# Two query tiles of 128 at the start of batch 0, with the other queries of that batch loaded later

## The chip, the cores and the metric

The kernel runs on one core of one Trainium2 chip. The metric is the device time of one execution in microseconds (us). Engines: PE is TensorE, DVE VectorE, ACT ScalarE, POOL GpSimd, SP SyncE.

## The reference

Block-sparse attention feeds a feed-forward layer. Shapes: q, k, v are 4 x 8 x 768 x 64 (batch, heads, sequence, head size), w_in is 512 x 2048, w_out 2048 x 512, all float32.

```python
scores = q @ k.T / sqrt(64)               # per batch and head
mask: neighbouring blocks of 32, first and last block, 3 random key blocks per query block
attn = softmax(where(mask, scores, -1e9)) @ v
x = attn, tokens x 512                    # 3072 tokens
out = relu(x @ w_in) ** 2 @ w_out
```

## The kernel before

Work goes by unit: two heads of one batch, so four units per batch, sixteen in all. A *slot* is one group of scores (256 queries, two key chunks of 128, two heads), with its exponential on ACT, its mask on DVE and its value matmuls on PE. When the four units of a batch have a query tile, the feed-forward layer ("hidden" matmuls with w_in, "output" matmuls with w_out) of these tokens can run. PE has some 258 us of matmuls, so the kernel is good in so far as PE is never without work.

The order of instructions on every engine is fixed when the kernel is built, by a list scheduler in Python. I call its result the **plan**. It always takes the task that can start first, by durations and arrival times that are written into the source. Nothing on the chip changes the order later: if the plan believes a load to be there and it comes later, the engine waits at that place.

The arrival times of batch 0, the weights, and the gates that hold batch 1 back behind weights (cut):

```python
    LEAD = 14                                   # casts of a later unit at most so far ahead
    PACE0, PACE, ... = 44, 1.313, ...           # slot s of batches 1..3 not before PACE0 + PACE * (s - first)
    ...
    load(0, (sy, sc_, sy)); load(1, (sc_, sy, sc_)); load(2, (sy, sc_, sy)); load(3, (sc_, sy, sy))
    ...
    def loads_gate(i, e):                       # a tiny DMA that reads weight chunk i, on the Sync queue
        src = w_in_sb[...] if i < NWP else w_out_sb[...]
        sy.dma_start(out=scratch[0:1, i % 4:i % 4 + 1], in_=src)
    ...
    arrive = [(6.2, 6.2, 8.4), (8.4, 10.5, 10.5), (12.5, 12.5, 13.6), (13.6, 15.2, 16.3)]   # q, k, v of units 0..3
    ...
        if u >= HP:                             # units of later batches: behind a gate
            g = gate[2] if u == HP else gate[5] if u == HP + 1 else gate[7]
            ld_t = T_(("SP", 1.3), s0 - 30, load, u, (sy, sy, sy), deps=... + [g], dma=4.0)
    ...
        if u == HP - 1:                         # weights: chunks 0..3 are w_in, 4..7 are w_out, 2.65 us each
            for i in range(2 * NWP):
                wl[i] = T_(("POOL", 0.85), -50 + i, w_load, i, after=12.6, late=2.2, dma=2.65)
            for i in (2, 5, 7):
                gate[i] = T_(("SP", 0.2), i, loads_gate, i, deps=[wl[i]], late=0.0)
```

The softmax here doesn't subtract the row's maximum and nothing guards it: scores larger than these inputs give would overflow.

Of the kernel before, what the change touches and what calls it, by code (L numbers as in the profile page):

```python
# [19 lines left out]
P = 128  # L20
# [5 lines left out]
def kernel(  # L26
# [31 lines left out]
    N_WARM = 12  # L58
# [21 lines left out]
    AHEAD = {"PE": 0, "DVE": 0, "ACT": 0.2, "POOL": 0.0, "SP": 0.0}  # L80
    LEAD = 14
    PACE0, PACE, SINGLE, MASK_AT = 44, 1.313, 1, 12.0
# [116 lines left out]

    sy, sc_ = nc.sync, nc.scalar  # L200
    sb_i = consts.tile([nb, n_rand * 2], I32, name="sb_i")
    sy.dma_start(out=sb_i, in_=sampled_blocks.bitcast(I32))
    load(0, (sy, sc_, sy))
    load(1, (sc_, sy, sc_))
    load(2, (sy, sc_, sy))
    load(3, (sc_, sy, sy))
# [7 lines left out]
    warm = consts.tile([P, 512], BF, name="warm")  # L214
# [7 lines left out]
    for _ in range(N_WARM):  # L222
        nc.tensor.matmul(junk, warm[:, 0:P], warm, start=True, stop=True)  # L223
# [7 lines left out]
    G.iota(row, pattern=[[0, 1]], base=0, channel_multiplier=1, **small)  # L231
    o3 = oh.rearrange("a (n p) -> a n p", p=P)
# [4 lines left out]
    identb = consts.tile([P, P], BF, name="identb")  # L237
    make_identity(nc, identb)
# [19 lines left out]
    A.copy(out=oh[D:P, :], in_=oh[0:D, :])  # L258
# [13 lines left out]
    def mask_rows(e):  # L272
        mtile["R"] = ps_s.tile([P, 1024], F32, name="pb", tag="ps")
        for c0 in (0, 512):
            w = min(512, S - c0)
            nc.tensor.matmul(mtile["R"][:, c0:c0 + w], bm, oh[0:nb, c0:c0 + w], start=True, stop=True)

    def mask_rows_evac(c0, c1, e):
        copy(e, R2[:, c0:c1], mtile["R"][:, c0:c1])
# [47 lines left out]

    def w_load(i, e):
        if i == 0:
            G.tensor_copy(out=held, in_=raw[2][1][0:1, 0, 0, 0:2])  # L330
        if i < NWP:
            fs = slice(i * d_ff // NWP, (i + 1) * d_ff // NWP)
            G.dma_start(out=w_in_sb[:, :, fs], in_=wiv[:, :, fs])
        else:
            ns = slice((i - NWP) * NF // NWP, (i - NWP + 1) * NF // NWP)
            G.dma_start(out=w_out_sb[:, ns, :], in_=wov[:, ns, :])
# [12 lines left out]
    def scores(slots, add, e):  # L349
        for a in slots:  # L350
            u, qi, cp = a
            i = u % NPB
            ps = ps_s.tile([P, 2, 2, QW], F32, name="ps", tag="ps")
            qsl = slice(qi * QW, (qi + 1) * QW)
            for c in range(2):
                ksl = slice((cp * 2 + c) * P, (cp * 2 + c + 1) * P)
                for h in range(2):
                    hs = slice(h * D, (h + 1) * D)
                    nc.tensor.matmul(ps[:, h, c, :], QK[i][hs, 1, ksl], QK[i][hs, 0, qsl],  # L359
                                     start=c == 0, stop=not add, skip_group_check=True)  # L360
                for h in range(2) if add else ():
                    hs = slice(h * D, (h + 1) * D)
                    nc.tensor.matmul(ps[:, h, c, :], oh[hs, ksl], R2[hs, qsl],  # L363
# [3 lines left out]
    def exps(a, e):  # L367
        pT = work.tile([P, 2, 2, QW], BF, name="pT", tag="pT", bufs=PT_BUFS)
        A.activation(out=pT, in_=stile.pop(a), func=AF.Exp, scale=scale)  # L369
        ptile[a] = pT  # L370

    def masks(a, e):
        u, qi, cp = a
        pT = ptile[a]
        m = MK[:, cp * 2:cp * 2 + 2, qi * QW:(qi + 1) * QW]
        V.tensor_tensor(out=pT, in0=pT, in1=m[:, None].broadcast_to([P, 2, 2, QW]), op=AOP.mult)  # L376

    def outs_of(t):
        return t[:, 0:4 * VW].rearrange("p (c h d) -> p c h d", h=2, d=VW)

    def values(a, e):
        u, qi, cp = a
        i = u % NPB
        pT = ptile.pop(a)
        if cp == 0:
            otile[u, qi] = ps_o.tile([P, 512], F32, name="po", tag="po")
        po = outs_of(otile[u, qi])
        for c in range(2):
            n = cp * 2 + c
            for qc in range(2):  # L390
                for h in range(2):
                    nc.tensor.matmul(po[:, qc, h, :], pT[:, h, c, qc * P:(qc + 1) * P], VT[i][:, h, n, 0:VW],  # L392
# [3 lines left out]
    def normalize(u, qi, e):  # L396
        po = outs_of(otile[u, qi])
        rs = work.tile([P, 2, 2, 1], F32, name="rs", tag="rs")
        V.reciprocal(out=rs, in_=po[:, :, :, D:VW])  # L399
        xq = work.tile([P, 2, 2, D], BF, name="xq", tag="xq", bufs=XQ_BUFS)  # L400
        V.tensor_tensor(out=xq, in0=po[:, :, :, 0:D], in1=rs.broadcast_to([P, 2, 2, D]), op=AOP.mult)  # L401
        xtile[u, qi] = xq

    def x_transp(u, qi, e):
        xq = xtile.pop((u, qi))
        pt = otile[u, qi][:, 384:512].bitcast(BF)
        for qc in range(2):
            nc.tensor.transpose(pt[:, qc * P:(qc + 1) * P], xq[:, qc].rearrange("p h d -> p (h d)"), identb)  # L408

    def x_evac(u, qi, e):  # L410
# [3 lines left out]
        copy(e, xT[b][:, a, qi * QW:(qi + 1) * QW], otile.pop((u, qi))[:, 384:512].bitcast(BF))  # L414

    def x_transp_dma(u, qi, e):
        b, a = divmod(u, HP)
        if b not in xT:
            xT[b] = work.tile([P, HP, S], BF, name="xT", tag="xT", bufs=XT_BUFS)
        sy.dma_start(out=xT[b][:, a, qi * QW:(qi + 1) * QW].rearrange("r (c p) -> r c p", p=P),  # L420
                     in_=xtile.pop((u, qi)).rearrange("p c h d -> p (c h d)"), transpose=True)
        otile.pop((u, qi))
# [4 lines left out]
    TILES = [(0, qi * QW, QW) for qi in range(NQ)]  # L427
    TILES += [(b, c0, S // 2) for b in range(1, B) for c0 in (0, S // 2)]
    NY = 8

    def hidden(T, f, half, e):
        b, c0, w = T
        if half == 0:
            htile[T, f] = ps_h.tile([P, TWM], F32, name="ph", tag="h")[:, 0:w]
        ph = htile[T, f]
        for kc in range(half * KM // 2, (half + 1) * KM // 2):
            nc.tensor.matmul(ph, w_in_sb[:, kc, f * P:(f + 1) * P], xT[b][:, kc, c0:c0 + w],  # L437
                             start=(kc == 0), stop=(kc == KM - 1))

    def relu(T, f, e):  # L440
        r = work.tile([P, TWM], F32, name="r", tag="r", bufs=R_BUFS)[:, 0:T[2]]
# [7 lines left out]
    def square(T, f, e):  # L449
        g = work.tile([P, TWM], BF, name="g", tag="g", bufs=G_BUFS)[:, 0:T[2]]  # L450
# [5 lines left out]
        gtile[T, f] = g  # L456
# [33 lines left out]
    def T_(engs, key, f, *args, **kw):  # L490
        return Task(engs, key, (lambda e: f(*args, e)), **kw)

    arrive = [(6.2, 6.2, 8.4), (8.4, 10.5, 10.5), (12.5, 12.5, 13.6), (13.6, 15.2, 16.3)]

    order = [(a, qi, cp) for qi in range(NQ) for a in range(HP) for cp in range(CP)]
    order += [(b * HP + a, qi, cp) for b in range(1, B) for qs in ((0, 1), (2,)) for a in range(HP) for qi in qs
              for cp in range(CP)]
    first = {}
    for s, (u, qi, cp) in enumerate(order):
        first.setdefault(u, s)  # L500
    ev, cv, tr, sc_of, va_of, mu, mk, wl, gate, xb = {}, {}, {}, {}, {}, {}, {}, {}, {}, {}

    def prepare(u):
# [5 lines left out]
        if u >= HP:  # L509
# [4 lines left out]
            for w in (1, 0):  # L514
                qc = Buf("qc")
                c = T_({"DVE": 0.55, "POOL": 1.2}, 101, cast_qk, u, w, slice(0, NCH), bias={"POOL": 0.5}, get=[qc], port=True,
                       after=PACE0 + PACE * (s0 - HP * NQ * CP) - LEAD, **at)
                tr[u].append(c)
                ev[u][w, 0] = ev[u][w, 2] = T_(("SP", 1.0), s0 - 10, transp_dma, u, w, deps=[c] + old_s, put=[qc], dma=1.2)
        else:  # L520
            at = dict(after=arrive[u][2])
            for ns in (slice(0, 2), slice(2, NCH)) if u == 0 else (slice(0, NCH),):
                n = ns.stop - ns.start
                for w in (0, 1):
                    qc, hb = Buf("qc"), Buf("h")
                    opts = {"ACT": 0.23 + 0.1 * n} if u == 0 and w else {"DVE": 0.07 + 0.08 * n}
                    if u:
                        opts["POOL"] = 1.2
                    c = T_(opts, s0 - 6 + ns.start, cast_qk, u, w, ns, after=arrive[u][w], get=[qc], port=True)
                    tr[u].append(c)  # L530
# [162 lines left out]
```

## Time and profile before

| | before |
|---|---|
| time, median of 3 runs | 276.78 us (276.52 to 277.39) |
| span of the profiled run | 275.2 us |
| PE busy | 263.5 us, 96% |
| mean granted TensorE clock | 0.998 |

Full PE means that the opening decides.

The measure of this study is the **delay** that the prediction defines: the real start of every fourth slot's scores minus the PE work that stands ahead of it in PE's order, priced from the trace. In an idle-free stretch it is flat; a wait of PE raises it. So the delay at PE's end, plus PE's work, plus a tail of some 3 us, is the span. Narrow slots are counted by area, so that "slot 12", the twelfth, stands at the same amount of scores in all kernels. A delay is that of the one profiled execution, a time that of all executions.

### The profile page before, as it was taken

The page shows a single profiled execution, that of the slowest core. Times are in us where ns is not written, and L with a number is a line of the kernel's source. Part 1 is how long each engine was busy: PE and PEld are TensorE (multiplying, and loading weights), DVE is VectorE, ACT ScalarE, POOL GpSimd, SP SyncE. Part 2 cuts the span into 40 slices and gives each one's busy share as a digit, 9 for nine tenths or more (in the row PEclk, how much of TensorE's full clock was granted, in tenths as well). Part 3 has the DMA queues.
Part 4 walks back from the last instruction along what each step waited for, and adds up shares of the span by engine and source line. Part 5 has one row for each costly group of instructions (what it writes and reads, how often), then busy time and mean ns, then how long its engine had stood idle before and what let it go on. Part 6 is the DMA issues. An engine that isn't in the chain of part 4 may idle for free.

```text
span 275.2 us, 7001 instructions
## 1 busy us (share of the span) xinstructions
PE 263.5 (96%) x2812; PEld 156.7 (57%) x2850; DVE 198.0 (72%) x392; ACT 212.0 (77%) x315; POOL 77.3 (28%) x105
## 2 busy tenths in 40 slices
PE   7897999899999999999999999999999999999994
PEld 2565756567666655655555555555555655555543
DVE  6794799989989778898987768876876745444400
ACT  4688999899899799997898988889989743444311
POOL 4660655625441224453232420111110100010010
PEclk9999999999999999999999999999999999999999
DMA  7999997999979969413512611111022011111122
GB/s 251 376 233 206 267 278 252 262 280 285 318 104 255 206 174 247 154 57 69 117 48 48 137 21 50 57 21 49 12 60 58 12 48 39 40 38 38 40 76 76
DMA packets 50522, 36.89 MB, mean 134 GB/s; under 512 B 30906, under 2 KB 47546, under 8 KB 50490
## 3 DMA queue, kind: packets, MB, share of 16 engines
q1 hardware_dynamic: 44906, 30.29, 41.3%
q0 software_dynamic: 4224, 4.19, 9.2%
q10 hardware_dynamic: 1360, 1.97, 2.1%
q8 instruction: 22, 0.36, 0.5%
q14 instruction: 10, 0.08, 0.1%
HBM read 27.26 MB, written 6.29 MB: 122 GB/s over the span
## 4 chain that ended last, share of the span: by engine, by line
PE 87%; DVE 4%; ACT 3%; DMA 2%; issue 2%; POOL 1%; POOLq 0%; ACTq 0%
PE ph L437 28%; PE py L477 28%; PE po L392 14%; PE ps L359 12%; DMA vs<-in_v_dram 2%; ACT pT L369 2%; PE junk L223 2%; DVE pT L376 1%; PE pt L311 1%; DVE r L446 1%; POOL g L455 1%; DVE QK L182 1%; PE po L408 1%; PE ps L363 0%; ACT MK L291 0%
## 5 line engine op out<-in xcount | busy, mean ns | idle before, releaser
L369 ACT ACTIVATE pT<-ps 128x1024 bf16<-128x1024 f32 x144 | 139.2, 1022 | 9.0 <-PE ps L359 5.6
L437 PE MATMUL ph<-xT,w_in_sb 128*128 128x384 bf16 (+1 forms) x576 | 107.0, 308 | 0.2
L376 DVE TENSOR_TENSOR pT<-pT,MK 128x1024 bf16<-128x1024 bf16 x132 | 98.8, 769 | 10.5 <-ACT pT L369 10.3
L477 PE MATMUL py<-w_out_sb,g 128*128 128x512 bf16 (+1 forms) x362 | 96.2, 369 | 2.5 <-POOL g L455 0.9
L455 POOL TENSOR_TENSOR g<-r 128x256 bf16<-128x256 f32 (+1 forms) x59 | 50.0, 853 | 164.5 <-DVE r L446 134.6
L437 PEld LDWEIGHTS <-w_in_sb 128*128 128x128 bf16 x576 | 51.9, 97 | 33.0 <-issue 1.3
L446 DVE TENSOR_SCALAR r<-ph 128x384 f32<-128x384 f32 (+1 forms) x96 | 49.6, 519 | 28.5 <-PE ph L437 27.2
L453 ACT ACTIVATE g<-r 128x384 bf16<-128x384 f32 (+1 forms) x85 | 42.3, 501 | 29.2 <-DVE r L446 28.5
L392 PEld LDWEIGHTS <-pT 128*128 128x128 bf16 x1152 | 44.4, 98 | 22.4 <-issue 7.7
L392 PE MATMUL po<-VT,pT 128*128 128x65 bf16 x1152 | 53.9, 194 | 1.5 <-DVE xT L182 0.7
L477 PEld LDWEIGHTS <-g 128*128 128x128 bf16 x400 | 36.3, 97 | 24.7 <-POOL g L455 1.2
L359 PE MATMUL ps<-QK 64*128 64x256 bf16 x576 | 46.6, 272 | 0.1
L359 PEld LDWEIGHTS <-QK 64*128 64x128 bf16 x576 | 22.8, 94 | 24.1 <-issue 20.7
L444 ACT ACTIVATE r<-ph 128x384 f32<-128x384 f32 (+1 forms) x48 | 21.0, 445 | 5.3 <-PE ph L437 4.7
L401 DVE TENSOR_TENSOR xq<-po,rs 128x256 bf16<-128x256 f32 x48 | 20.4, 424 | 1.7
L399 DVE RECIPROCAL rs<-po 128x4 f32<-128x4 f32 x48 | 8.6, 180 | 17.9 <-PE po L392 17.6
L180 ACT COPY ys<-py 128x512 f32<-128x512 f32 (+1 forms) x21 | 11.9, 565 | 11.7 <-PE py L477 11.7
L182 POOL CAST VT<-vs 128x768 bf16<-128x768 f32 x15 | 13.5, 902 | 17.9 <-PE po L392 12.1
L182 DVE CAST qc<-ks 128x768 bf16<-128x768 f32 x14 | 9.5, 682 | 0.0
L182 DVE CAST qc<-qs 128x768 bf16<-128x768 f32 (+2 forms) x13 | 8.6, 666 | 0.8 <-DMA qs<-in_q_dram 0.8
L363 PE MATMUL ps<-R,oh 64*128 64x256 bf16 x48 | 5.9, 269 | 0.0
L223 PE MATMUL junk<-warm 128*128 128x512 bf16 x12 | 4.2, 528 | 1.5 <-DVE warm L215 1.5
(52 smaller groups left out, 61.3 us busy)
## 6 DMA issues: line engine op xcount, KB each, us to landing
out_dram<-ys SPq DMA_DIRECT2D x23, 256.0 KB, 2.2
vs<-in_v_dram SPq DMA_DIRECT2D x15, 384.0 KB, 6.4
qs<-in_q_dram SPq DMA_DIRECT2D x14, 384.0 KB, 4.5
ks<-in_k_dram SPq DMA_DIRECT2D x14, 384.0 KB, 6.4
w_in_sb<-in_moe_w_in_dram POOLq DMA_DIRECT2D x4, 512.0 KB, 10.1
w_out_sb<-in_moe_w_out_dram POOLq DMA_DIRECT2D x4, 512.0 KB, 20.7
ks<-in_k_dram ACTq DMA_DIRECT2D x2, 384.0 KB, 6.0
qs<-in_q_dram ACTq DMA_DIRECT2D x2, 384.0 KB, 5.0
```

What stands on the lines that cost most here:

```text
L182: (V if e == "DVE" else G).tensor_copy(out=out, in_=in_)
L359: nc.tensor.matmul(ps[:, h, c, :], QK[i][hs, 1, ksl], QK[i][hs, 0, qsl], start=c == 0, stop=not add, skip_group_check=True)
L369: A.activation(out=pT, in_=stile.pop(a), func=AF.Exp, scale=scale)
L376: V.tensor_tensor(out=pT, in0=pT, in1=m[:, None].broadcast_to([P, 2, 2, QW]), op=AOP.mult)
L392: nc.tensor.matmul(po[:, qc, h, :], pT[:, h, c, qc * P:(qc + 1) * P], VT[i][:, h, n, 0:VW], start=(n == 0 and qc == 0 and h == 0), stop=n ...
L401: V.tensor_tensor(out=xq, in0=po[:, :, :, 0:D], in1=rs.broadcast_to([P, 2, 2, D]), op=AOP.mult)
L437: nc.tensor.matmul(ph, w_in_sb[:, kc, f * P:(f + 1) * P], xT[b][:, kc, c0:c0 + w], start=(kc == 0), stop=(kc == KM - 1))
L444: A.activation(out=r, in_=src, func=AF.Relu)
L446: V.tensor_scalar(out=r, in0=src, scalar1=0.0, scalar2=None, op0=AOP.max)
L453: A.activation(out=g, in_=r, func=AF.Square)
L455: (G if e == "POOL" else V).tensor_mul(out=g, in0=r, in1=r)
L477: nc.tensor.matmul(ytile[T, i], gtile[T, f][:, ts * P:(ts + 1) * P], w_out_sb[:, f, cs[0]:cs[1]], start=(f == 0), stop=(f == NF - 1))
```

## The change

The intent: start earlier and have feed-forward work for PE earlier. The first 256 queries of batch 0 are treated as two tiles of 128, each slot with three key chunks instead of two; their feed-forward work can start after eight short slots. So that they come early, only these queries are loaded with the keys and values; the remaining 512 queries of the four units (**late queries** below) are loaded behind the values of unit 3, beside the weights. With it go the plan's arrival times, its pace, and a number that sends more squares to GpSimd. The core (warm-up, order of constants, generalised helper functions cut):

```diff
-    AHEAD = {"PE": 0, "DVE": 0, "ACT": 0.2, "POOL": 0.0, "SP": 0.0}
-    LEAD = 14
-    PACE0, PACE, SINGLE, MASK_AT = 44, 1.313, 1, 12.0
+    AHEAD = {"PE": 0.05, "DVE": 0, "ACT": 0.2, "POOL": 0.0, "SP": 0.0}
+    LEAD = 8
+    PACE0, PACE, SINGLE, MASK_AT = 36, 1.611, 1, 12.0
...
-    load(0, (sy, sc_, sy))
-    load(1, (sc_, sy, sc_))
-    load(2, (sy, sc_, sy))
-    load(3, (sc_, sy, sy))
+    for eng, u, w, ns in ((sc_, 0, 1, KEYS[0]), (sy, 0, 0, QRS[0]), (sc_, 1, 1, ALL), (sy, 0, 1, KEYS[1]),
+                          (sc_, 1, 0, QRS[0]), (sy, 0, 2, ALL), (sc_, 1, 2, ALL), (sy, 2, 1, ALL),
+                          (sy, 2, 0, QRS[0]), (sy, 3, 1, ALL), (sy, 3, 0, QRS[0]), (sy, 2, 2, ALL), (sy, 3, 2, ALL)):
+        load_part(eng, u, w, ns)
...
+    def load_rest(e):
+        sy.dma_start(out=scratch[0:1, 3:4], in_=raw[HP - 1][2][0:1, 0, 0, 0:1].bitcast(BF)[:, 0:1])
+        for u in range(HP):
+            load_part(sy, u, 0, QRS[1])
...
-    TILES = [(0, qi * QW, QW) for qi in range(NQ)]
+    QT = {0: [(0, P), (P, P)] + [(c0, QW) for c0 in range(QW, S, QW)]}
+    QT.update({b: [(c0, QW) for c0 in range(0, S, QW)] for b in range(1, B)})
+    TILES = [(0, c0, w) for c0, w in QT[0]]
...
-    arrive = [(6.2, 6.2, 8.4), (8.4, 10.5, 10.5), (12.5, 12.5, 13.6), (13.6, 15.2, 16.3)]
+    arrive = {(0, 1, 0): 4.3, (0, 0, 0): 4.4, (0, 1, CP): 5.3, (0, 2, 0): 7.4, (1, 1, 0): 6.7, (1, 0, 0): 7.4, (1, 2, 0): 9.5,
+              (2, 1, 0): 9.6, (2, 0, 0): 10.0, (3, 1, 0): 11.1, (3, 0, 0): 11.5, (2, 2, 0): 12.5, (3, 2, 0): 13.5}
+    arrive.update({(u, 0, 2): 17.0 + 0.9 * u for u in range(HP)})      # the late queries
...
+            T_(("SP", 2.0), -60, load_rest, after=13.5)
             for i in range(2 * NWP):
-                wl[i] = T_(("POOL", 0.85), -50 + i, w_load, i, after=12.6, late=2.2, dma=2.65)
+                wl[i] = T_(("POOL", 0.85), -50 + i, w_load, i, after=9.6 + 2.6 * i, late=1.3, dma=3.9 if i in (1, 2) else 2.6)
...
-                sq_of[x] = T_(SQ[w], n_key, square, t, f, deps=[rr], get=[gb], put=[rb], bias={"ACT": 0.2})
+                sq = T_(SQ[w], n_key, square, t, f, deps=[rr], get=[gb], put=[rb], bias={"ACT": 0.7})
```

## The prediction

> **What bounds the kernel now.** I read the busy shares first, then the chain of waits over the whole span, then the chain in the opening, then the DMA queues.
>
> From the page (busy us, share of the span, instructions; then the share of each engine in 40 slices of 6.9 us):
>
> ```profile
> PE 263.5 (96%) x2812; PEld 156.7 (57%) x2850; DVE 198.0 (72%) x392; ACT 212.0 (77%) x315; POOL 77.3 (28%) x105
> ...
> PE   7897999899999999999999999999999999999994
> ...
> DMA  7999997999979969413512611111022011111122
> ```
>
> PE is full from about 55 us on; its weak slices are the first eight, and there DMA is full too. A stretch of the chain of waits at 140 us (start, us, what) shows what "full" means:
>
> ```profile
> 141.14 0.86 PE py L477 x4
> 142.00 0.65 PE ph L437 x4
> 142.65 0.54 PE ps L359 x8
> ...
> 145.73 0.54 PE ps L359 x8
> 146.28 0.59 PE po L392 x16
> ```
>
> Pieces follow each other without a gap. They give PE's price list: an output matmul (512 columns) 0.215 us, a hidden one (384 columns) 0.162, a two-slot score group 0.54 and its 16 value matmuls 0.59, both including the change between 64-row and 128-row use of the array. Hidden matmuls of 256 columns start 0.109 apart in the timeline, transposes 0.056.
>
> I priced both PE instruction orders with this list (score matmuls in concurrent pairs; score and value groups split so that they give the 0.54 and 0.59 above, about 0.115 per change of row mode). Before: 258.5 us of PE work. Comparing the running sum with the real start of every fourth slot's scores gives a **delay** (real time minus PE work due so far): 7.7 us at slot 4, 8.2 at slot 12, 10.5 at slot 24, 13.0 at slot 36, and then 12.95 to 13.0 for all 108 slots left. So after 55 us nothing but PE work counts, and span = 258.5 + 13.0 + 3.5 (last copy and store; PE ends at 271.7 of 275.2) = 275.0, against 275.2 measured. The change can gain only by lowering the final delay.
>
> What sets the last step of the delay is in the chain at 43 to 56 us:
>
> ```profile
> 43.72 5.91 DMA vs<-in_v_dram
> ...
> 49.78 0.82 POOL VT L182
> 50.60 1.07 POOL g L455
> ...
> 51.72 0.39 PE py L477
> ```
>
> Values of the third unit of batch 1 land at 49.6, GpSimd waits for them before it makes a square that an output matmul needs. Those loads were held back behind the weights by gates, small DMAs that the Sync queue issues once a weight chunk has landed:
>
> ```profile
> 23.88 0.25 SPq L343 DMA_DIRECT2D scratch<-w_in_sb  x1
> ...
> 34.69 0.24 SPq L343 DMA_DIRECT2D scratch<-w_out_sb  x1
> ...
> 41.39 0.24 SPq L343 DMA_DIRECT2D scratch<-w_out_sb  x1
> ```
>
> So the third w_in chunk was there at 23.9, the second w_out chunk at 34.7, the fourth at 41.4. The opening is bound by DMA. Its rates: 378 GB/s in 4 to 14 us (Sync and Scalar queues alone), 207 in 16 to 26 (weights alone, counted as written), and in 28 to 35 us both queues together:
>
> ```profile
> DMA packets 1530, 1.89 MB, mean 270 GB/s; under 512 B 51, under 2 KB 1530, under 8 KB 1530
> ...
> q0 software_dynamic: 765, 0.76, 64.1%
> q1 hardware_dynamic: 765, 1.13, 51.5%
> ```
>
> Packet for packet: each gets 765 packets, so weights fall to 0.11 MB/us and loads to 0.16 MB/us.
>
> **What the Trainium skill says.** "TensorE: Matmul & The Clock Gate", Back-to-back issue gap, has a warm gap of N/2.4 + 2.5 ns: 216 ns for 512 columns, 56 for 128. The trace agrees (215 and 56). The same page, Step-by-step: what each phase is for, says that matmuls stay in program order; so one waiting output matmul holds all later PE work. "DMA: Bandwidth & Descriptors", Queues, rings and completion order, says the engines alternate between queue rows at packet granularity; the 765 and 765 above agree. Its Specifications table asks for at least 512 B per transfer for line rate: the new query loads have runs of exactly 512 B (two chunks of 64 floats) where the old had 1536; no run shows yet what that costs.
>
> **The change part by part.**
>
> *Warm-up and first loads.* 12 junk matmuls of 512 become 14 of 256 (4.2 us become about 3.0), the identity is built earlier, and the first keys and queries are 196 and 131 KB instead of 393 KB each. First scores now start at 8.1 us, first exponential at 8.8. I expect about 6.5 and 7.3. Keys and values of batch 0 with a third of its queries are 3.67 MB instead of 4.72 MB, which at 0.38 MB/us is 2.8 us less ahead of the weights.
>
> *Two tiles of 128.* For the first 256 queries 12 exponentials of 1024 elements become 16 of 768: back to back 0.90 us each in the timeline, about 0.68 for 768 (my estimate by elements), so 10.8 and 10.9 us: even. MoE work can start after 8 short exponentials instead of 12 long ones. PE: 96 score and mask matmuls of 256 become 192 of 128, 64 hidden ones become 128 of half the width, four more single groups change row mode twice: the new order prices at 259.4 us, 1.0 more.
>
> *The order.* Hidden work stands earlier. In the order before, the first output matmul comes after 20.4 us of PE work and the first that needs the second w_out chunk after 25.7. In the new order they come after 21.1 and **22.7**. At the delay of 6 to 7 us that the better opening would leave, PE would be at the latter at about 29 us.
>
> *The weights.* This is where I think it sticks. The bytes that move until the second w_out chunk is in are the same: 4.72 MB of batch 0 (12.4 us), six weight chunks of 0.524 MB (15.3 us at 0.205), and the share that unit 4's loads take. Unit 4's loads still wait for the third w_in chunk, which I put at 24.4 (remaining queries, 1.05 MB, now share with the weights), and flow some 3 us later, from 27.2. With DMA from 2.2 us, and about 0.8 us empty between the end of the early loads (12 us) and the first weight packets (issue at 9.7 plus the 3.1 us seen before): T = 2.2 + 12.4 + 0.8 + 15.3 + 0.42(T - 27.2), where 0.42 = 0.16/0.38; T = 33.2. The same sum for before (no empty stretch, loads from 26.8) gives 32.1, and the landing was 34.7, 2.5 later. So **35.7 us** for the new landing. GpSimd's order adds a risk of up to 2 us: it issues w_out chunks only behind a cast of late-loaded queries. I take 36.0.
>
> *Sum.* Output matmul at 36.0; PE work from there 259.4 - 22.7 = 236.7; tail 3.5; 0.4 for new waits of PE on ScalarE between slots 24 and 40, where both have 5 to 6 us of work per four slots. Together 276.6 us of span; the timed median lies 1.5 above the span of before (276.78 against 275.24), so 278.1. The final delay would be about 13.7, against 13.0. Since I may have put the landing too late (not before 34.5, the bytes say), and tuned numbers of the change (pace, lead) speak for a trial that paid, I move to 277.5.
>
> **The rivals.**
>
> *The opening's gain survives.* If the weights come by 31 us, the delay is about 9 and the span 259.4 + 9 + 3.5 = 272, time 273.5 (1.2% faster). For it: the third unit's values, which set the end before, no longer do (their square is needed after 46.1 us of PE work, when 5.6 us of delay would do), PE starts earlier, ScalarE has fewer gaps. Against it: bytes ahead of the second w_out chunk are unchanged and DMA was already full from 2 to 35 us.
>
> *ScalarE as the bound.* First exponential at 7.3, and ScalarE's own work up to slot 40 is 48.4 us (0.90 per long and 0.68 per short exponential, plus relus, squares and copies in its order): 55.7 us, where PE has 52.3 us of work plus its delay. It binds only if the delay is under 3.4. Not likely.
>
> *Small packets and narrow matmuls.* If 512 B runs go at half rate, the early queries (0.52 MB) cost 1.4 us more and all later landings shift: 279. Score pairs of 128 that take 80 ns instead of 58 cost 2.1 us, but before the wait, so nothing.
>
> *Slower pace of batches 1 to 3* (1.611 instead of 1.313 per slot): slots end after 205.6 us of work instead of 202.4; PE is full either way. Zero.
>
> **Range and chances.** The landing may lie between 34.5 and 38, which makes 276.5 to 280 before the pull towards a gain; the first rival pulls the low end to 273.8. Faster by 2% needs 271.2, a delay of 6.8: not with output matmuls at 22.7 waiting for a chunk later than 30 us. Chances: faster 0.07, within 2% 0.88, slower 0.05.
>
> **What would show it.** Right: the first exponential is near 7.3; hidden matmuls start by 18 to 20 us instead of 27.6; PE has one gap of several us near 30 to 36 that ends with the second w_out chunk; after that the delay is flat; PE's last matmul is about 236 us after the end of the gap. Wrong: no such gap (the chunk is there by 31), or a delay that goes on growing after 56 us. If the gap is there but the chunk lands at 33, I am 2 to 3 us too slow; if GpSimd's cast holds the issue, 2 us too fast.

## More of the kernel before

The stretches of the kernel before, with busy time of each engine (and its instructions), then the granted clock of PE, the share of DMA and its rate:

```profile
core 0: us, PE busy (x) PEld busy (x) DVE busy (x) ACT busy (x) POOL busy (x), PEclk, DMA share, GB/s
...
7.00:10.00 3.00, 2.23 (x32) 1.42 (x33) 2.20 (x6) 1.35 (x3) 1.76 (x2) 1.00 1.06 380
10.00:15.00 5.00, 4.81 (x74) 2.99 (x73) 3.85 (x10) 4.51 (x6) 4.08 (x7) 1.00 1.07 366
15.00:20.00 5.00, 4.66 (x75) 2.98 (x71) 4.66 (x11) 3.70 (x6) 3.35 (x5) 1.00 1.24 209
20.00:25.00 5.00, 4.44 (x83) 3.00 (x80) 1.62 (x5) 4.48 (x6) 0.00 (x0) 1.00 1.24 207
25.00:30.00 5.00, 4.08 (x61) 2.67 (x58) 3.73 (x8) 4.41 (x8) 1.13 (x2) 1.00 1.20 234
30.00:35.00 5.00, 4.95 (x69) 3.67 (x68) 3.91 (x10) 4.97 (x10) 3.78 (x5) 1.00 1.16 270
```

PE is busy for 4.1 to 5.0 of every 5 us from 10 us on, DMA is full, and the clock is 1.00 throughout. (The clock's records begin only with its first change to full, at 4.6 us here; what lies before it is counted as full in the column and in the means, so a clock of 1.00 there says nothing.)

## The result, and the profile after

| | before | after |
|---|---|---|
| time, median | 277.08 us (276.52 to 277.86, 4 runs) | 285.1 us (283.98 to 286.98, 4 runs) |
| span of the profiled run | 275.2 us | 282.3 us |
| mean granted clock | 0.998 | 0.982 |
| delay at slots 4 / 8 / 12 | 7.7 / 8.2 / 8.2 us | 8.8 / 10.4 / 16.5 us |
| delay at slots 20 / 28 / 40 | 10.5 / 11.6 / 13.0 us | 16.5 / 17.4 / 17.9 us |
| delay at slot 80, and at PE's end | 13.0, 13.3 us | 19.1, 19.7 us |

All outputs are right. The ratio of the times is 1.029, with a 95% interval of 1.022 to 1.037: slower by over 2%. Here and below a ratio is the mean time of one kernel's runs over that of the kernel before in the same rounds, so not quite the ratio of the medians quoted. The span grew by 7.0 us: 1.0 of PE work (259.4 instead of 258.5), 6.4 of delay, and 0.4 less of tail. The difference in delay is 1.1 us at slot 4, 2.2 at slot 8 and 8.3 at slot 12. Later the kernel before waits more than the changed one, so that 4.9 are left at slot 40 and 6.4 at the end. By far the largest step lies between slots 8 and 12.

The page of the changed kernel: busy shares, PE's share and the granted clock in 40 slices of 7.1 us.

```profile
PE 265.8 (94%) x2973; PEld 162.6 (58%) x3012; DVE 199.6 (71%) x391; ACT 190.8 (68%) x277; POOL 142.4 (50%) x166
...
PE   5884999899999999999999999999999999999995
...
PEclk9797799999999999999999999999999999999999
```

PE's weakest slice is the fourth, 21 to 28 us, and the clock falls in the second, fourth and fifth. The same stretches as above, after:

```profile
core 0: us, PE busy (x) PEld busy (x) DVE busy (x) ACT busy (x) POOL busy (x), PEclk, DMA share, GB/s
...
7.00:10.00 3.00, 2.79 (x41) 2.44 (x42) 1.03 (x4) 2.15 (x4) 1.80 (x4) 0.57 1.07 360
10.00:15.00 5.00, 4.19 (x88) 3.28 (x85) 4.74 (x14) 2.60 (x5) 3.63 (x5) 0.91 1.15 294
15.00:20.00 5.00, 4.39 (x84) 2.80 (x80) 1.97 (x5) 4.98 (x9) 1.03 (x2) 1.00 1.20 241
20.00:25.00 5.00, 1.82 (x33) 1.30 (x33) 2.15 (x6) 1.66 (x3) 0.00 (x0) 0.95 1.18 244
25.00:30.00 5.00, 3.49 (x46) 2.65 (x48) 1.86 (x6) 1.41 (x3) 2.03 (x3) 0.50 0.99 241
```

From 20 to 30 us PE is busy 5.3 us instead of 8.5, and most of that is at half clock. DVE, ACT and POOL are busy for 4.0, 3.1 and 2.0 of these 10 us, while DMA stays about as full as before (1.18 and 0.99, against 1.24 and 1.20). What PE waits for, in its timeline of these 10 us (start, busy time, and in brackets the idle time before it with its releaser):

```profile
20.65 0.40 PE L321 MATMUL pt<-identb,qc 128*128 128x128 bf16 x4 [1.25 <-DVE qc L182]
...
23.41 0.38 PE L321 MATMUL pt<-identb,qc 128*128 128x128 bf16 x4 [1.92 <-DVE MK L303]
...
25.75 0.61 PE L321 MATMUL pt<-identb,qc 128*128 128x128 bf16 x4 [1.36 <-POOL qc L182]
```

These are groups of four transposes, for four chunks of 128 queries: the late queries of units 0, 1 and 2. (The releaser of the second is the one that came last by the profile: a mask copy at 22.67, which frees a buffer in PSUM and which stood on DVE behind the cast at 22.33.) The timeline of DVE shows that the casts ahead of them wait for the loads:

```profile
20.16 0.43 DVE L182 CAST qc<-qs 128x512 bf16<-128x512 f32 x1 [1.91 <-DMA qs<-in_q_dram]
22.33 0.43 DVE L182 CAST qc<-qs 128x512 bf16<-128x512 f32 x1 [1.74 <-DMA qs<-in_q_dram]
...
26.75 0.62 DVE L182 CAST qc<-qs 128x512 bf16<-128x512 f32 x1 [2.67 <-DMA qs<-in_q_dram]
```

GpSimd casts those of unit 2, and holds two weight chunks behind it:

```profile
25.08 0.61 POOL L182 CAST qc<-qs 128x512 bf16<-128x512 f32 x1 [9.06 <-DMA qs<-in_q_dram]
25.64 1.48 POOL L351 DMA_DIRECT2D w_out_sb<-in_moe_w_out_dram  x2
```

The first two w_out chunks were issued at 25.6; the kernel before issued all four from 14.5 on. The Sync queue of the changed kernel has the late loads behind their gate, and the gates of the third w_in and the second w_out chunk:

```profile
13.74 0.25 SPq L339 DMA_DIRECT2D scratch<-vs  x1
14.04 1.93 SPq L208 DMA_DIRECT2D qs<-in_q_dram  x4
24.75 0.24 SPq L358 DMA_DIRECT2D scratch<-w_in_sb  x1
...
38.44 0.24 SPq L358 DMA_DIRECT2D scratch<-w_out_sb  x1
```

The second w_out chunk lands at 38.4 instead of 34.7. And the chain of waits goes straight through the late queries of unit 3:

```profile
15.47 11.25 DMA qs<-in_q_dram
26.75 0.62 DVE qc L182
```

This load of 256 KB takes 11.3 us from its issue. It stands behind the other late queries on its queue, and the weights move at the same time: in 16 to 27 us the packets of the weights' queue take 78% of the time of the 16 DMA engines, those of the loads' queue 38%. The build of the kernel can be made to print what the plan believed. Set beside the trace:

| data | the plan of after | landed in after |
|---|---|---|
| late queries of units 0, 1, 2, 3 | 17.0, 17.9, 18.8, 19.7 us | 20.2, 22.3, 25.1, 26.8 us |
| second w_out chunk | 31.8 us | 38.4 us |

The kernel before believed 33.3 for the second w_out chunk and got it at 34.7. So the plan of the changed kernel is out of step in two places, by 3 to 7 us each.

The opening itself brought little. The first scores start at 7.5 us against 8.1, yet at slot 4 the delay is 1.1 us larger. The first exponential starts at 8.34, against 8.77. On ACT stands, ahead of the first scores' last copy, a cast of unit 0's second keys, which the plan expected at 5.3:

```profile
6.38 0.51 ACT L180 CAST qc<-ks 128x384 bf16<-128x384 f32 x1 [1.12 <-DMA ks<-in_k_dram]
6.80 0.36 ACT L180 COPY QK<-pt 128x256 bf16<-128x256 bf16 x1
7.58 0.48 ACT L180 COPY QK<-pt 128x384 bf16<-128x384 bf16 x1 [0.42 <-PE pt L321]
8.34 1.51 ACT L385 ACTIVATE pT<-ps 128x768 bf16<-128x768 f32 x2 [0.28 <-PE ps L378]
```

The clock is a second reason, which no run tests. From 7.5 to 10.9 us PE ran at half clock (0.57 in the stretch from 7 to 10 us), where the kernel before has 1.00. The change had also shortened the warm-up, from 12 junk matmuls of 512 columns to 14 of 256; in the 3.4 us ahead of the drop PE was busy 45%. h2_after, the changed kernel again, drops at the same place (8.1 to 11.5 us). So a part of the delay at slot 4 may be the warm-up's.

### The profile page after: what moved, and what is told of

It is laid out like the page before. It is cut to its first block, busy times and chain, and to the rows that moved or that the text cites.

```text
span 282.3 us, 7437 instructions
## 1 busy us (share of the span) xinstructions
PE 265.8 (94%) x2973; PEld 162.6 (58%) x3012; DVE 199.6 (71%) x391; ACT 190.8 (68%) x277; POOL 142.4 (50%) x166
## 4 chain that ended last, share of the span: by engine, by line
PE 68%; DMA 12%; DVE 9%; issue 3%; SPq 3%; POOL 2%; ACT 2%; ACTq 0%; DVEq 0%; POOLq 0%
PE py L502 25%; PE ph L461 23%; PE po L407 10%; PE ps L374 9%; DVE pT L392 5%; DMA vs<-in_v_dram 4%; DMA qs<-in_q_dram 4%; DMA ks<-in_k_dram 3%; DMA xT<-xq 1%; SPq L197 1%; DVE qc L182 1%; DVE xq L417 1%; POOL g L479 1%; DVE r L470 1%; SPq L208 1%
## 5 line engine op out<-in xcount | busy, mean ns | idle before, releaser
L479 POOL TENSOR_TENSOR g<-r 128x384 bf16<-128x384 f32 (+1 forms) x120 | 114.4, 960 | 101.3 <-DVE r L470 67.0
L385 ACT ACTIVATE pT<-ps 128x1024 bf16<-128x1024 f32 (+1 forms) x148 | 140.5, 1003 | 27.3 <-PE ps L374 17.9
L392 DVE TENSOR_TENSOR pT<-pT,MK 128x1024 bf16<-128x1024 bf16 x132 | 105.5, 816 | 9.6 <-ACT pT L385 9.2
L461 PE MATMUL ph<-xT,w_in_sb 128*128 128x384 bf16 (+2 forms) x640 | 108.2, 294 | 0.1
L470 DVE TENSOR_SCALAR r<-ph 128x384 f32<-128x384 f32 (+1 forms) x81 | 42.2, 523 | 31.9 <-PE ph L461 19.4
L374 PE MATMUL ps<-QK 64*128 64x256 bf16 (+1 forms) x624 | 48.7, 268 | 0.2
L180 ACT COPY ys<-py 128x512 f32<-128x512 f32 (+1 forms) x24 | 13.7, 570 | 48.2 <-PE py L502 40.8
L374 PEld LDWEIGHTS <-QK 64*128 64x128 bf16 x624 | 25.6, 96 | 24.0 <-issue 20.6
L468 ACT ACTIVATE r<-ph 128x384 f32<-128x384 f32 (+1 forms) x63 | 27.4, 452 | 6.2 <-PE ph L461 5.0
L182 POOL CAST VT<-vs 128x768 bf16<-128x768 f32 x16 | 15.4, 967 | 15.8 <-PE po L407 10.5
L417 DVE TENSOR_TENSOR xq<-po,rs 128x256 bf16<-128x256 f32 (+1 forms) x52 | 21.0, 404 | 1.8
L415 DVE RECIPROCAL rs<-po 128x4 f32<-128x4 f32 (+1 forms) x52 | 9.1, 175 | 13.1 <-PE po L407 12.8
L477 ACT ACTIVATE g<-r 128x384 bf16<-128x384 f32 (+1 forms) x24 | 11.5, 479 | 1.4 <-DVE r L470 0.8
```

What stands on the lines that cost most here:

```text
L180: A.copy(out=out, in_=in_)
L182: (V if e == "DVE" else G).tensor_copy(out=out, in_=in_)
L374: nc.tensor.matmul(ps[:, h, j * w:(j + 1) * w], QK[i][hs, 1, ksl], QK[i][hs, 0, qsl], start=j == 0, stop=not add, skip_group_check=True)
L385: A.activation(out=pT[:, :, 0:n], in_=stile.pop(a)[:, :, 0:n], func=AF.Exp, scale=scale)
L392: V.tensor_tensor(out=pT, in0=pT, in1=m[:, None].broadcast_to([P, 2, len(cs), w]), op=AOP.mult)
L417: V.tensor_tensor(out=xq, in0=po[:, :, :, 0:D], in1=rs.broadcast_to([P, n, 2, D]), op=AOP.mult)
```

## The experiments

The first theory was that PE's wait for the late queries is the loss. Rivals were: narrow tiles, the drop of the clock, the placing of the output work against the second w_out chunk, GpSimd's squares, and the pace. The shortened warm-up was not tested.

### Late queries loaded early; one tile; true arrivals; clock filled

**e1_nogate** issues the late queries right behind the other loads. The plan's numbers, and so all orders of computation, are left as they were.

```diff
+    for u in range(HP):
+        load_part(sy, u, 0, QRS[1])                 # at the end of the first loads
     def load_rest(e):
-        sy.dma_start(out=scratch[0:1, 3:4], in_=raw[HP - 1][2][...])
-        for u in range(HP):
-            load_part(sy, u, 0, QRS[1])
+        pass
```

> The late queries are issued right behind the values of unit 3 instead of after their landing; all compute engines keep the changed kernel's order. Theory A (late queries share DMA with the weights, land at 20 to 27 us and hold PE and GpSimd): they land by about 16 us, the PE gaps between 19 and 30 us go, the clock stays full after 11 us, the delay of PE at slot 12 falls from 16.5 to about 10, the second w_out chunk lands near 35 us and the time is 278 to 280 us. Rival B (narrow tiles, more squares on GpSimd and the other pace cost the time): 284 us or more.

Measured: 282.66 us (280.53 to 283.18), ratio 1.016 (1.011 to 1.022), between the two expectations. The gaps between slots 8 and 12 are gone: the delay is 8.8 at slot 8 and 8.7 at slot 12. But it jumps to 14.7 at slot 20. The chain of waits shows the new place:

```profile
19.86 16.30 DMA w_out_sb<-in_moe_w_out_dram
36.20 1.01 PE py L502 x2
```

PE stands before an output matmul for the second w_out chunk, which lands at 36.2. (Right behind this wait PE ran at half clock, from 36.1 to 39.5 us; that the clock stays full after 11 us was a miss.) So the late queries are a real wait, of which only a third came back, because a second wait stood behind it.

**e2_tile256** keeps the late loads but treats the first 256 queries as one tile.

```diff
-    QT = {0: [(0, P), (P, P)] + [(c0, QW) for c0 in range(QW, S, QW)]}
+    QT = {0: [(c0, QW) for c0 in range(0, S, QW)]}
```

> The first 256 queries are one tile again, the late loads stay. Theory A: the late queries still land at 20 to 27 us and hold PE, so 281 to 285 us. Rival B (the narrow tiles cost it): 278 us or less.

Measured: 287.23 us (287.08 to 287.68), ratio 1.034 (1.032 to 1.037); delay 16.8 at slot 16, 24.1 at the end. That is above both expectations. Taking the narrow tiles away makes it slower, so they aren't the cause.

**e3_order** leaves the loads and tells the plan when the late queries really come.

```diff
-    arrive.update({(u, 0, 2): 17.0 + 0.9 * u for u in range(HP)})
+    arrive.update({(u, 0, 2): (20.2, 22.3, 25.1, 26.8)[u] for u in range(HP)})
```

> Loads as in the changed kernel, but the scheduler is told the measured arrival of the late queries (20.2, 22.3, 25.1, 26.8 us), so it puts other work ahead of their transposes. Theory A': it is the order of PE that turns the late landing into a loss: hidden work fills the gap, delay at slot 12 smaller, 279 to 282 us. If the landing itself is the loss because GpSimd's cast still holds the w_out chunks to 38 us: 283 to 285 us.

Measured: 283.42 us (282.93 to 284.66), ratio 1.021 (1.018 to 1.025). The delay is 9.4 at slot 12 and 15.0 at slot 20: as with early loads, the first wait goes and the second takes its place. The time lies in the second expectation's range, but not for its reason: with the true arrivals the plan gives all casts of late queries to DVE, GpSimd issues the first two w_out chunks at 16.1 us and not at 25.6, and the second still lands only at 36.9.

**e4_fill** puts eight junk matmuls of 256 columns ahead of each group of late transposes, to keep PE busy for the clock's sake.

```diff
     def transp(u, w, ns, e):
+        if w == 0 and ns.start == 2 and u < HP:
+            fill = ps_y.tile([P, d_model], F32, name="fill", tag="y")
+            for _ in range(8):
+                nc.tensor.matmul(fill[:, 0:256], warm[:, 0:P], warm, start=True, stop=True)
```

> Eight junk matmuls of 256 columns stand ahead of each late transpose of queries, 0.9 us per unit, while PE waits there 1.3 to 1.9 us. If the half clock from 24.5 to 31.3 us costs time of its own: the clock stays full there and the time falls by 1.5 to 3 us to 282 to 283.5, and the runs spread less. If only the landing counts: 285 as it was.

Measured: 284.49 us (283.95 to 285.76), ratio 1.025 (1.021 to 1.029). The clock still halved, at 29.1 to 32.5 us instead of 24.5 to 31.3, and the delay was 17.9 at slot 12. The run is inconclusive on what the clock costs; it doesn't speak for the clock as the main cause.

### What stands behind the first wait

All three start from e1_nogate. **e5_gate** keeps the loads of batch 1 behind later weight chunks, so that the w_out chunks come earlier:

```diff
-            g = gate[2] if u == HP else gate[5] if u == HP + 1 else gate[7]
+            g = gate[5] if u == HP else gate[6] if u == HP + 1 else gate[7]
-            for i in (2, 5, 7):
+            for i in (5, 6, 7):
```

> Early late-queries as in e1_nogate, and the loads of batch 1 wait for w_out chunks 2, 3 and 4 instead of w_in chunk 3 and w_out chunks 2 and 4, so they do not share DMA with the chunk that PE waits for. Theory: the wait of e1_nogate (second w_out chunk at 36.2 us, delay 14.7 at slot 20) is the share of unit 4's loads: the chunk lands near 33.8 us, the delay at slot 20 is about 12 and the time 280 to 281 us. If the landing is not what counts: 282.7 as e1_nogate.

Measured: 278.77 us (278.52 to 279.65), ratio 1.004 (1.002 to 1.005). A larger gain than expected (280 to 281 us). The gate of the second w_out chunk on the Sync queue went at 33.3, and the delay at slot 20 was 10.5, not 12:

```profile
33.25 0.25 SPq L358 DMA_DIRECT2D scratch<-w_out_sb  x1
```

**e6_bias** undoes the number that sends squares to GpSimd.

```diff
-  ... square, ... bias={"ACT": 0.7})
+  ... square, ... bias={"ACT": 0.2})
```

> e1_nogate with the squares' old bias (51 squares on GpSimd instead of 120, as before had 59). Its order has 26.25 us of PE work ahead of the second w_out chunk instead of 22.7, so the wait there should leave a delay of about 10 (36.2 - 26.25). If GpSimd's squares slow VectorE's masks (0.82 against 0.77 us) and so cause the growth of the delay after slot 24 (2.7 us in e1_nogate), the growth falls under 1.5 us: 275 to 277 us in all. If they do not: growth 2.7, 277 to 279 us.

Measured: 278.99 us (278.73 to 279.57), ratio 1.004 (1.002 to 1.006). GpSimd has 51 squares instead of 120. But the new order also puts the output matmul of the second w_out chunk after 26.3 us of PE work and not 22.7, so most of the gain (delay 9.8 at slot 20) is that. After slot 20 the delay still grows, to 14.1. The squares are not the cause of that growth.

**e7_wtrue** tells the plan that the first two w_out chunks take longer, and changes nothing else.

```diff
-  dma=3.9 if i in (1, 2) else 2.6)
+  dma=3.9 if i in (1, 2) else 4.4 if i in (4, 5) else 2.6)
```

> e1_nogate, with the scheduler told that the first two w_out chunks come 1.8 us later each. Its order has 26.5 us of PE work ahead of the second w_out chunk; the loads are the same, so the chunk lands at 36 again and the delay there is about 10 instead of 14.7. With the growth of e1_nogate (2.7): 277 to 279 us. If the order is not what counts, 282.7.

Measured: 278.31 us (276.8 to 279.8), ratio 1.001 (0.999 to 1.003). The plan now believes 35.4 for the second chunk, which lands at 35.7; delay 9.1 at slot 20, 13.0 at slot 28, 13.7 at slot 144. Against e1_nogate one number gave 4.4 us.

### The two waits together

**e8_alltrue** is the changed kernel with the code of its late loads and gates untouched, and both corrections of e3_order and e7_wtrue in the plan.

> The loads of the changed kernel untouched (late queries behind the landing of the values); the scheduler is told the measured arrival of the late queries and that w_out comes later. If the loss is the scheduler's wrong arrivals rather than the loads: PE's gaps at 20 to 30 us go as in e3_order (delay 9.5 at slot 12), the second w_out chunk (at about 38 us, held by GpSimd's cast) stands after 26.25 us of work: delay about 12, time 278 to 280 us, against 283.4 for e3_order.

Measured: 279.43 us (278.91 to 279.8), ratio 1.005 (1.003 to 1.007). The second w_out chunk came at 37.2 and the late queries when they had before; but the casts of these on DVE, the first and the last of which stand here, have no wait ahead of them now:

```profile
21.40 0.42 DVE L182 CAST qc<-qs 128x512 bf16<-128x512 f32 x1
...
30.59 0.64 DVE L182 CAST qc<-qs 128x512 bf16<-128x512 f32 x1
```

The delay was 10.0 at slot 12, 10.7 at slot 20, 14.8 at slot 144. The clock had no drop after 12.6 us, where its records begin; but just before that PE was at half clock, for the pairs of score matmuls of 128 columns start 0.107 us apart from 8.4 to 12.5 us and 0.056 from 15 us on. So 5.7 us of the loss came back by changing five numbers of the plan (by the medians; by the ratios it is 1.9% to 2.4%, with h2_after below or the first result as the changed kernel).

The loads were not changed, but the new plan does move the issue of two weight chunks. As in e3_order no cast stands ahead of them on GpSimd:

```profile
16.55 1.50 POOL L351 DMA_DIRECT2D w_out_sb<-in_moe_w_out_dram  x2
```

Issued 9 us earlier than in the changed kernel, the second w_out chunk lands 1.2 us earlier (37.2, where the expectation had 38). Up to 1.2 of the 5.7 us may be that, and not the order of PE (an estimate from the two landings).

**h1_wonly** has the correction for the weights alone, in the changed kernel; **h2_after** is the changed kernel again, in the same rounds. (In the texts of this and of g2_truepace "third" and "fourth pair of weight chunks" both mean the first two w_out chunks.)

> The changed kernel with one number altered: the scheduler is told that the third pair of weight chunks takes longer, so that the first output matmul of the second w_out chunk stands after 26.5 us of PE work and not 22.7. First theory, two misplaced waits hide each other: the late queries still hold PE to a delay of some 16.4 us at slot 12, which is later than the second wait, so the new place gains nothing: 284 to 285.5 us. Rival, the w_out place alone is the loss (as it is where the late queries do not hold PE, 282.7 to 278.3 us): 279 to 281 us.

> The changed kernel itself again, beside the run with the one number altered, so that both have rounds on the same chip: 284 to 286 us, delay 16 to 17 us from slot 12, two stretches of half clock before 32 us. If the half clock is a matter of chance, it is in other places or absent.

Measured: h1_wonly 284.95 us (284.4 to 286.84), ratio 1.026 (1.024 to 1.029); h2_after 284.28 us (283.5 to 285.12), ratio 1.024 (1.021 to 1.027). The correction that is worth 4 us elsewhere is worth nothing here. In the changed kernel PE comes to the second w_out chunk after 22.7 us of work and 16.5 of delay, so at 39.2, when the chunk (38.4) is already there; moving that place saves no wait. In h2_after the half clock came in the same two places (8.1 to 11.5 and 25.1 to 32.0 us), so it is hardly chance. In h1_wonly, whose profiled execution was its slowest (286.84), the transposes wait as in the changed kernel, and so do the w_out chunks behind GpSimd's cast (issued at 26.3, the second landed at 38.0):

```profile
20.66 0.40 PE L321 MATMUL pt<-identb,qc 128*128 128x128 bf16 x4 [1.30 <-DVE qc L182]
...
23.44 0.38 PE L321 MATMUL pt<-identb,qc 128*128 128x128 bf16 x4 [1.94 <-DVE MK L303]
...
26.39 0.61 PE L321 MATMUL pt<-identb,qc 128*128 128x128 bf16 x4 [1.97 <-POOL qc L182]
```

Together (medians in us, ratio to before):

| | w_out chunks told as in the change | told later |
|---|---|---|
| late queries, told as in the change | 285.1 (1.029); again 284.28 (1.024) | 284.95 (1.026) |
| late queries, told true | 283.42 (1.021) | 279.43 (1.005) |
| queries loaded early | 282.66 (1.016) | 278.31 (1.001) |

Either correction alone brings 0 to 1.7 us, both bring 5.7 (4.9 against h2_after). The two misplaced waits lie one behind the other, and each hides the other.

### Tiles and pace

**f1_best** is e5_gate with true arrivals for unit 0's second keys (6.8) and values (8.2) and for the weights.

```diff
-  (0, 1, CP): 5.3, (0, 2, 0): 7.4,
+  (0, 1, CP): 6.8, (0, 2, 0): 8.2,
-  dma=3.9 if i in (1, 2) else 2.6)
+  dma=3.9 if i in (1, 2, 7) else 3.3 if i in (4, 5) else 2.6)
```

> e5_gate (late queries early, batch 1 gated behind w_out) with the scheduler told the arrivals that the traces show for the first keys and values and for the weights. The second w_out chunk (at 33.3 us) stands after 25.4 us of PE work instead of 22.7, and unit 0's second keys no longer block ScalarE. Theory (all losses are waits for loads that the order expects too early): delay about 8 to 8.5 at slot 4, 9 to 9.5 at slot 20, then a growth of 2.5 to 3.5 as in e5_gate and e7_wtrue: 276.5 to 277.5 us, level with before or a little under it. If the narrow tiles cost time by themselves: above 279.

Measured: 279.99 us (279.64 to 280.38), ratio 1.008 (1.006 to 1.010): a miss. The opening was as hoped, with a delay of 7.9 at slot 4 and 8.4 at slot 20, where before has 10.5. But after that it grew in small steps to 14.6. The opening's gain was given back.

**f2_pace** is f1_best with the pace, lead and allowance of the kernel before.

```diff
-    AHEAD = {"PE": 0.05, ...}
-    LEAD = 8
-    PACE0, PACE, ... = 36, 1.611, ...
+    AHEAD = {"PE": 0, ...}
+    LEAD = 14
+    PACE0, PACE, ... = 44, 1.313, ...
```

> f1_best with the old pace, lead and look-ahead of before. If the new pace causes the growth of the delay after slot 24: delay flat from slot 40 on, 275 to 276.5 us. If it does not: as f1_best within 0.5 us, or slower.

Measured: **275.64 us** (275.49 to 276.66), ratio 0.993 (0.991 to 0.995): faster than both kernels, by 0.7% against before. Delay 8.2 at slot 20, 9.5 at slot 40, 10.4 at slot 144. What PE waits for between 34 and 90 us, with the new pace (f1_best; busy time, mean ns, idle time before and its releasers):

```profile
L407 PE MATMUL po<-VT,pT 128*128 128x65 bf16 x312 | 14.5, 194 | 1.2 <-DVE pT L392 1.1
...
L424 PE MATMUL po<-identb,xq 128*128 128x128 bf16 x16 | 2.2, 221 | 1.0 <-DVE xq L417 0.8
```

and with the old (f2_pace):

```profile
L407 PE MATMUL po<-VT,pT 128*128 128x65 bf16 x328 | 15.7, 194 | 0.8 <-DVE pT L392 0.7
...
L424 PE MATMUL po<-identb,xq 128*128 128x128 bf16 x16 | 2.2, 220 | 0.0
```

Under the slower pace PE waits longer for masks and normalised values of DVE, at most 0.8 us at a time. These two lines differ by 1.4 us, and from 35 to 120 us PE is busy 1.9 us less; that is less than half of the 4.3 us by which the times differ. The rest was not traced. The clock is not it: both profiled runs are at full clock from 10.0 us on.

The same three numbers were then taken out of the changed kernel alone (**g1_pace**), out of e8_alltrue (**g2_truepace**), and put alone into the kernel before (**g4_beforepace**):

> The changed kernel with only the three numbers of the pace put back (allowance for PE, lead of the casts, start and step of the later batches). First theory, the loss of the changed kernel comes from its opening (the late queries and the order made for arrivals that do not hold) and the pace only adds to it: the delay of PE at slot 20 stays near 16.5 us, the growth after it shrinks from 3.2 us to some 1 to 2, and the time falls to about 281 to 283 us, still slower than before. Rival, the pace is the whole loss: delay at the end under 14 and 277 us. A third, the pace has no effect in this kernel (what the prediction called zero): 285 us.

> The changed kernel with its loads as they are, the true arrivals of the late queries and of the fourth pair of weight chunks told to the scheduler, and the pace of the kernel before. First theory, the scheduler's numbers are all of the loss: delay some 10.7 us at slot 20 as in the run with the true numbers alone, growth cut from 4.1 to under 2, and 275.5 to 277.5 us, so at or below the kernel before with the late loads untouched. Rival, the late loads cost something by themselves: 278 us or more, as with the true numbers alone (279.4).

> The kernel before with nothing but the new pace. If the pace costs by itself what it cost in the best version (4.3 us), 280 to 281.5 us, with the delay growing from some 13 us at slot 40 by 3 to 4 us. If it costs only together with the changed squares and narrow tiles, within 1 us of 277.5. The prediction's own reading (zero) is the second.

| | new pace | old pace |
|---|---|---|
| kernel before | g4: 280.73 us, 1.008 (1.005 to 1.011) | 1 |
| changed kernel | 1.029, again 1.024 | g1: 284.05 us, 1.022 (1.019 to 1.025) |
| with true numbers | e8: 279.43 us, 1.005 (1.003 to 1.007) | g2: 278.32 us, 1.002 (1.001 to 1.003) |
| best loads | f1: 279.99 us, 1.008 (1.006 to 1.010) | f2: 275.64 us, 0.993 (0.991 to 0.995) |

In the kernel before the new pace alone costs 0.8%; there the delay grows to 15.0 at slot 44 and 16.6 at slot 72, where before stays at 13.0. (About 1.2 of that stands there at slot 4 already, too early for the pace: the profiled run came to full clock at 7.4 us, that of the kernel before at 4.6.) In the changed kernel it can't be told from nothing: the intervals overlap, the delay at slot 20 is the same 16.6, and my expectation of 281 to 283 us missed. My reading, which no run tests, is that PE is so late there that the other engines have time in hand. g2_truepace came out at 278.3, a little over the 275.5 to 277.5 that I had expected and in the range of the rival (278 or more): with true numbers and the old pace the change's own loads are 0.2% slower than before, no better.

**The narrow tiles** were replaced by one of 256 in three more settings: in e8_alltrue (**f3_256true**), in f1_best (**f4_256best**) and in f2_pace (**g3_256pace**).

> e8_alltrue (loads of the changed kernel, true arrivals of queries and weights) with one tile of 256 instead of two of 128. If the two narrow tiles have a value of their own (filler for PE sooner): 1 to 2 us slower than e8_alltrue's 279.4, so 280.5 to 281.5. If they have none: 278 to 279.5.

> f1_best with one tile of 256. PE work is 258.5 instead of 259.9 us. If the narrow tiles have a value of their own: 1 to 2 us slower than f1_best; if none: 1 us faster.

> The fastest version so far (275.6 us) with the first tile of batch 0 as one tile of 256 queries again. If the narrow tiles are worth what they were meant for (the first output matmuls wait for fewer hidden tiles), this is slower than 275.6 by 1 us or more. If they only add PE work (259.9 against 258.5 us), it is faster by about 1.4 us: 274 us.

| | two tiles of 128 | one of 256 |
|---|---|---|
| changed kernel | 285.1 us, 1.029 | e2: 287.23 us, 1.034 (1.032 to 1.037) |
| with true numbers | e8: 279.43 us, 1.005 (1.003 to 1.007) | f3: 279.42 us, 1.005 (1.003 to 1.008) |
| best loads, new pace | f1: 279.99 us, 1.008 (1.006 to 1.010) | f4: 277.99 us, 1.001 (1.000 to 1.003) |
| best loads, old pace | f2: 275.64 us, 0.993 (0.991 to 0.995) | g3: 277.43 us, 0.999 (0.997 to 1.000) |

By the medians (f2 and g3 are of different rounds; their ratios say 1.6 us) the narrow tiles are worth 1.8 us in the fastest version, and cost 2.0 with the new pace. g3_256pace was expected at 274 us if the tiles only added work, and missed that. They have no value of their own here, only one within a plan.

## Why the prediction was wrong

**The bound and its measure held.** After slot 80 the delay of the changed kernel is flat (19.1 to 19.1 at slot 144), and the longer span is PE work plus delay, as the prediction adds it up. So what was wrong is the delay: 13.7 predicted, 19.7 measured.

**The step that failed is "The weights. This is where I think it sticks."** It took the second w_out chunk for the only wait that the new order meets, and the late queries only for bytes that share the DMA, with "a risk of up to 2 us" through GpSimd. It never asked what the plan does with the late queries' arrival times, 17.0 to 19.7. The same sum of bytes could have told: at 14.0 to 16.0 they are issued, 1.05 MB; at the 0.16 MB/us that the prediction itself reads for loads beside weights, they need at least 6.6 us of flow (an estimate), so the last could not be there at 19.7. In the trace they land at 20.2 to 26.8, and PE, whose order is fixed, stops before their transposes. That raises the delay by 6.1 between slots 8 and 12, where that of the kernel before doesn't move, and leaves the changed kernel 8.3 behind. (Up to PE's end the kernel before then loses 5.1 us more and the changed one 3.2, hence 6.4.) Some of it is the clock: from 20 to 30 us PE is idle 4.7 us (10 less 1.82 and 3.49 busy), and 3.49 us of work ran at half clock, which is 1.7 us more (an estimate; the ends of PE's work are modelled). The prediction didn't consider the clock at all. What it costs by itself stayed open in e4_fill. The step "The order" failed with it: it has PE at the output matmul of the second w_out chunk at about 29 us, at a delay of 6 to 7; PE came there at 39.2, at a delay of 16.5, and the chunk was there.

**The wait that was predicted is real, one layer below.** With the late queries early (e1_nogate) PE does what the prediction says: a gap that ends with the second w_out chunk, at 36.2, where 36.0 was taken. That the two agree so closely is in part luck, for the loads are not those that the sum was made for. The delay is then 14.7, not 13.7, and it goes on growing to 17.4; even so the time is 282.7 and not 277.5. In the changed kernel itself the chunk came at 38.4. The prediction's own sentence, "if GpSimd's cast holds the issue, 2 us too fast", is what happened: the issue at 25.6 is held by the cast at 25.08. Where no cast holds it (e3_order, e8_alltrue) the chunk landed at 36.9 and 37.2, which puts the hold at 1.2 to 1.5 of the 2.4 us (an estimate).

**"Slower pace ... Zero" was wrong as a rule.** It argued that PE is full either way. In the kernel before that pace costs 0.8%, in the best version 4.3 us, less than half of it in small waits of PE that the trace shows. In the changed kernel putting the pace back brings 0.2 to 1.1 us by the medians, not clear of noise, so this is a second error, not the cause. The prediction's own sign for it, "a delay that goes on growing after 56 us", did show: 17.9 at slot 40, 19.1 at slot 80.

**The opening's gain was over-rated.** First scores at 7.5 and first exponential at 8.3, where 6.5 and 7.3 were expected, since the second keys came a microsecond after the plan's 5.3. Then PE ran at half clock to 10.9 us, which the prediction didn't consider when it counted the shorter warm-up as a gain. Hidden matmuls start at 30.8, behind the late queries, where 18 to 20 was expected.

**What held.** PE's extra 1.0 us of work. Packets of 512 B hurt little: in the packet records of the changed kernel they took 28.8 ns on the mean, and those of 1536 B in the same first 14 us 70.4, so 17.8 against 21.8 bytes per ns. And ScalarE was not the bound.

**What stays open.** Why the delay grows by 4 us after slot 20 in e8_alltrue; what the half clock costs apart from the waits that bring it; what the shortened warm-up costs; and which of the pace's three numbers matters. The lists of executions bear on the clock: of 19 of e7_wtrue the four with a mean clock of 1.00 took 276.8 to 277.0 us, the median of the others (0.988 to 0.994) is 278.7; in e1_nogate the one at 1.00 took 280.5, the others 282.3 to 283.2. So half clock goes with some 1.8 us or more there; whether it makes them or comes from the same longer waits, no run shows.

## What to carry to other kernels

When a change moves a load to a later time, look first for whoever consumes it in a fixed order, compare the plan's arrival time with the bytes that must flow until then, and only then count what its bytes do to others. Where two waits lie one behind the other, mending either alone shows nothing: test both together before a cause is ruled out. A new order should be tuned anew against the arrival times that its own trace shows; here corrected numbers alone brought 5.7 us, up to 1.2 of it perhaps because weights then came earlier.

## What the Trainium skill lacked or had wrong

- "TensorE: Matmul & The Clock Gate", HAM oscillation — how this bites in real kernels, gives the rule that there should be no idle gaps of PE over about 3.4 us. Here the clock halved without such a gap: in the changed kernel after 3.4 us in which PE was busy 40%, with a longest gap of 1.9 us. In eleven of the runs there are 18 such drops in the first 60 us; in the 3.4 us ahead of each PE was busy between 14% and 60%, and the longest gap was 0.8 to 3.0 us. Stretches of the same length with 60 to 64% busy, in four of these runs, kept the full clock, so in these runs the limit lies near 60%. The page's next section knows that frequent short idles make the clock swing, but no section has a busy share. Its window of 3413 ns, in the section What's actually happening, agrees: the half-clock stretches lasted 3.4, 6.8 or 10.2 us.
- "DMA: Bandwidth & Descriptors", Specifications, has 512 B as the smallest transfer for line rate. At exactly 512 B the packets here moved 17.8 bytes per ns and at 1536 B in the same 14 us 21.8, so 512 B was 18% short.
- No page that I looked up says what sharing between queues does to the latency of one load: 256 KB of queries, issued at 15.5 us behind other queries and beside weights from GpSimd's queue, took 11.3 us to land, while the median of the loads of 384 KB of queries over the whole run is 4.4 us.
- Nor does one say how to place work in a fixed order against loads whose arrival is uncertain, which decided this (5.7 us).
